# A transformer layer on one core: splitting the second chunk of 512 queries into two of 256

## The chip, the core and the metric

The kernel runs on one core of a Trainium2 chip. The core has a matrix engine (TensorE, PE in the profile, with its weight loads as PEld), a vector engine (VectorE, DVE), an activation engine (ScalarE, ACT), a general engine (GpSimd, POOL) and a queue that only issues transfers (SyncE, SP). The metric is device time in microseconds (us).

## The reference

The reference is one pre-norm transformer layer on 2048 tokens of width 640, in bfloat16: 32 attention heads of 20 columns, then a gated MLP of width 1728.

```python
qkv = (x @ wqkv).reshape(B, S, 3, H, Dh) ...          # S 2048, D 640, H 32, Dh 20
scores = einsum("bhqd,bhkd->bhqk", q, k) * Dh ** -0.5
o = einsum("bhqk,bhkd->bhqd", softmax(scores), v)
attn = o.reshape(B, S, D) @ wo
h = x + A(layernorm(x))                                # A: attention as above
h2 = h + (gelu(n @ w_gate) * (n @ w_up)) @ w_down      # n = layernorm(h), width 1728
```

## The kernel before

**Chunks and slots.** The queries are cut into chunks (`SIZES`, L308): 512, 512, 256, 256, 256, 128 and 128. The heads are in 8 groups of 4. A slot is the work of one 512-wide block of query columns: one group for a 512 chunk, two groups at once for a 256 chunk, four for a 128 chunk. So there are always 32 slots, 8 for a chunk of 512, 4 for one of 256 and 2 for one of 128.

**Tiles.** A score tile is 128 partitions (keys) by 512 columns in one PSUM bank, and belongs to one head. The four heads of a group lie in four groups of 32 rows of PE (index `j`, `tile_position=(32 * j, 0)` in `qk_mms`, L913), and four tiles with the same place are a quad. A slot has 64 tiles, 2048 in all. For 512 queries a tile is one matmul of 512 columns, for 256 queries two of 256, for 128 four of 128.

**Two exponentials.** Most tiles go to ACT, several banks in one `ACTIVATE` (L945). Some quads (`D_QUADS`, L323: 1 to 3 a slot, 68 quads or 272 tiles in all) go to DVE, which reads a tile out of PSUM (L852) and computes the exponential by a chain of six integer and half-precision operations (L863 to L868, in the helper's line L354 in the profile) on two tiles at once, or on four from slot 18 on. 1776 tiles are left for ACT.

**Units and banks.** A unit is what one `ACTIVATE` takes. `PAT` (L798) gives the banks: banks 0 to 2 and 3 to 4 in turn, so that units have three and two tiles, except in chunk 1, where banks 0 to 2 and 3 to 5 are used. There a unit that also carries a DVE tile has two tiles for ACT and puts the DVE tile in its third bank ("six"). Elsewhere the DVE tile gets a bank of its own out of `BG[c]` (L1156): the banks of 7, 5 and 4 that `PAT` leaves. That is bank 7 alone in chunk 1, and 7 and 5 elsewhere. The DVE tiles are taken in a fixed order (`dq`, L793), row groups 0, 1, 2, 3 of a quad one after the other, whatever row groups the tiles of the unit use.

**Values.** The products with v (`pv_op`, L875) gather in bank 6. At the end of a slot `epilogue` (L997) copies the bank out (`osb`), transposes it, divides, and writes `o_nat`.

**After a chunk.** `post(c, ...)` (L1036) does the rest for the queries of a chunk: transposes, the output projection (L640), the residual (L1057), layernorm statistics and apply, then for each 512 columns a gate matmul (L1089) with its copy out of PSUM (L1124), GELU on ACT for the whole chunk at once (`after=cp`), the up matmul (L1089 again) with its product (L1135), and the down matmul (L1146) with its residual sum (L1150) and the output transfer. It runs in the gaps of the next chunk, in the banks `BG[c + 1]`. The GELU uses another function table of ACT than exp, so each chunk costs a table load before and one after. The last chunk is the `tail`, with all banks and GELU bank by bank (L1111). Chunks share buffers: `base(c)` (L991) gives the first of four row tiles (`h_sb`, `o_nat`, `hnT`, and the stretch of `ha_f` from `hb`). A chunk of 512 takes all four, the chunks of 256 take 0 to 1 or 2 to 3 in turn. A chunk's `post` therefore waits until the chunk that held its tiles before has read them for the last time.

**Order of the work.** Nothing is queued by hand: `Sched` (L44) is a list scheduler in the program that simulates the engines with fixed costs and writes out a fixed order for each engine. Priorities (L329 to L330): scores 0, values 1, `P_EPI` 2 (the DVE exponential too), `P_LN` 2.5 (projection and layernorm of `post`), `P_BG` 3 (its MLP); among equals the earlier chunk goes first. DVE operations that free a bank have at most 1.8. GELU on ACT has -1. PE is filled with idle matmuls (L354, `ps<-kt_all,zer`) where the planner finds it too quiet. The planner takes 0.215 us for a unit's scores and 0.08 us for a DVE tile's, whichever row groups they use.

Of the kernel before, what the change touches and what calls it, by code (L numbers as in the profile page):

```python
# [304 lines left out]
NT = S // 128  # L305
NA = D // 128
NG = H // 4
SIZES = (512, 512, 256, 256, 256, 128, 128)  # L308
CHUNKS = tuple((sum(SIZES[:i]), n) for i, n in enumerate(SIZES))
NF = (DFF + 127) // 128  # L310
F0 = tuple(min(128 * f, DFF - 128) for f in range(NF))
# [16 lines left out]

P_EV = 1.8  # L329
P_QK, P_PV, P_PRO, P_EPI, P_LN, P_BG = 0, 1, 1.5, 2, 2.5, 3  # L330


def bass_sequential_preLN__mha_block__glu_gated_geglu__prompt_kernel(
# [12 lines left out]
    with ExitStack() as es:  # L346
# [16 lines left out]
        def c_dve(n, rate=1.0625):  # L363
            return 0.061 + n * rate * 1e-3
# [208 lines left out]
        def ln_apply(eng, src, dst, dkey, t, rkeys, prio):  # L573
            if eng == "act":
                fn = I("activation", dst, src, ACT.Identity, bias=nm[:, t:t + 1], scale=rs[:, t:t + 1])
            else:
                fn = I("tensor_scalar", dst, src, mu[:, t:t + 1], rs[:, t:t + 1], ALU.subtract, ALU.mult)
            return op(eng, fn, 0.82 if eng == "act" else c_dve(D, 0.46), prio,
                      reads=list(rkeys) + [("mu", t), ("rs", t)] + ([("nm", t)] if eng == "act" else []), writes=[dkey])
# [215 lines left out]
            tiles += rest  # L795
            slot_end.append(len(tiles))

        PAT = [((0, 1, 2), (3, 4, 5)) if c in (1,) else ((0, 1, 2), (3, 4)) for c in range(len(CHUNKS))]  # L798
        units, ubank, dtile, begins = [], [], [], []
        i, di = 0, 0  # L800
        while i < len(tiles):
            bs = PAT[slots[tiles[i][0]][0]][len(units) % 2]
            six = len(PAT[slots[tiles[i][0]][0]][1]) == 3
            xd = None
            if di < len(dq) and dq[di][0] <= i:
                xd = dq[di][1]
                di += 1
            n = len(bs) - (1 if six and xd else 0)
            units.append(tiles[i:i + n])
            begins.append(i)  # L810
            ubank.append(bs[0])
            dtile.append(xd)
            i += len(units[-1])
        assert di == len(dq)
        d_quad = {}
        for u, x in enumerate(dtile):
            if x:
# [12 lines left out]
        exp_ops = []  # L830
        p_next = [0]

        def d_exp(b, tile, prio, u):

            c = slots[tile[0]][0]
            kind = "e" if c == 0 else "l" if tile[0] < D_WIDE else "w"
            n = 4 if kind == "w" else 2
            h = len(d_raw)
            if h == 0:
                busy = set(x[1][1] for x in d_done)  # L840
                pool = [(kind, i) for i in range(5 if kind != "w" or slots[units[u][0][0]][0] > 3 else 3)]
                pool = [p for p in pool if p not in busy]
                assert pool
                d_cur[0] = min(pool, key=lambda p: d_last.get(p, -1))
                d_last[d_cur[0]] = len(d_ops)
            i = d_cur[0]
            v = {"e": dv0, "l": dv, "w": dvw}[kind][i[1]]
            df, dw = {"e": (df0, dw0), "l": (df1, dw1), "w": (df2, dw2)}[kind]
            keys = [("dv", i)] + ([("dv", ("l", k)) for k in ((0, 1), (2, 3), ())[i[1]]] if kind == "w" and i[1] < 3 else [])
            aft = tuple(e_ops) + (tuple(last_qk[0]) if c else ()) + (tuple(last_qk[1]) + tuple(d_late) if kind == "w" else ()) + \  # L850
                (tuple(last_qk[2]) + tuple(last_qk[3]) if kind == "w" and i[1] > 2 else ())
            d_ops.append(op("dve", lambda eng: eng.tensor_scalar(v[:, 512 * h:512 * h + 512], bank(b), EXP_MUL, -32000.0,  # L852
                                                                 ALU.mult, ALU.max), c_dve(512), P_QK,
                            reads=[("SD", tile)], writes=keys, rel=[b], after=aft))
            d_raw.append(tile)
            if kind != "w":
                d_late[:] = d_ops[-8:]
            if h < n - 1:
                return
            zi = df.bitcast(I16)  # L860
            w_ = len(d_raw) / 2
            d = lambda fn, n, r, w: d_ops.append(op("dve", fn, 0.066 + n * w_, prio, reads=r, writes=w))
            d(I("tensor_scalar", zi, v, 511, 2048, ALU.bitwise_and, ALU.bitwise_or), 0.265, [("dv", i)], ["df"])  # L863
            d(I("tensor_scalar", dw, zi, CA / OCT, CB, ALU.mult, ALU.add), 0.265, ["df"], ["dw"])
            d(I("tensor_tensor", dw, dw, dw, ALU.mult), 0.53, ["dw"], ["dw"])
            d(I("tensor_tensor", dw, dw, zi, ALU.mult), 0.53, ["df", "dw"], ["dw"])
            d(I("tensor_tensor", v, v, dw, ALU.add), 0.53, ["dw", ("dv", i)], [("dv", i)])
            d(I("tensor_scalar", v, v, 0.25, 16256.0 + 128.0 * (CC - 1.0), ALU.mult, ALU.add), 0.265, [("dv", i)], [("dv", i)])  # L868
            if kind != "w":
                d_late[:] = d_ops[-8:]  # L870
            for k, tl in enumerate(d_raw):
                d_done.append((v[:, 512 * k:512 * k + 512].bitcast(BF16), ("dv", i), tl))
            d_raw.clear()
# [115 lines left out]


        def base(c):  # L991
            n = CHUNKS[c][1]
            if n == 128:
                return 2 + (c == len(CHUNKS) - 1)
            return 2 * (c % 2) if n < 512 else 0

        def epilogue(s_, bk):  # L997
            s = s_ % 2
# [35 lines left out]
               after=tuple(e_ops) + tuple(w_readers) if c == 0 else ())  # L1034

        def post(c, banks, tail):  # L1036
            p = P_EPI if tail else P_LN
            q0, nq = CHUNKS[c]
            nt = nq // 128
            tb = base(c)  # L1040
# [2 lines left out]
            for tt in range(tb, tb + nt):  # L1043
                t = q0 // 128 + tt - tb
                i = t % 2
                if tail or c == 0:
                    transposes(o_nat[:, tt, :], [("on", g, tt) for g in range(NG)], oT[:, :, tt * 128:(tt + 1) * 128],
                               ("hnT", tt), banks, P_EPI, "act" if tail else "dve", after=first)
                else:
                    dma_transposes(o_nat[:, tt, :], [("on", g, tt) for g in range(NG)], oT[:, :, tt * 128:(tt + 1) * 128],  # L1050
                                   ("hnT", tt), after=first)
                for hf in range(2):
                    bk = Bank(*banks)
                    key = ("bk", sc_id())
                    list(chain(bk, key, 320, [(oT[:, a, tt * 128:(tt + 1) * 128], wo[:, a, hf * 320:(hf + 1) * 320])
                                              for a in range(NA)], [("hnT", tt), "wo"], p, after=(sc.lw[("h", tt, hf)],)))
                    op("dve", lambda eng, bk=bk, tt=tt, hf=hf, i=i: eng.tensor_tensor(  # L1057
                        h_sb[:, tt, hf * 320:(hf + 1) * 320], bank(bk, 320), h_sb[:, tt, hf * 320:(hf + 1) * 320], ALU.add),
                       c_dve(320), p, reads=[key, ("h", tt, hf)], writes=[("h", tt, hf)], rel=[bk], after=first)
                ln_stats(h_sb[:, tt, :], t, [("h", tt, 0), ("h", tt, 1)], p)  # L1060
            if tail:
                op("act", I("activation", nm[:, 0:1], off0[:, 0:1], ACT.Sqrt), 0.2, -1, mode="sqrt", reads=["off0"],
                   writes=["warmsq"], after=(exp_ops[-1],))
            ln_rsqrt(q0 // 128, nt, p, table=tail)
            if tail:
                op("act", I("activation", nm[:, 1:2], off0[:, 0:1], ACT.Gelu_apprx_tanh), 0.2, -1, mode="gelu",
                   reads=["off0"], writes=["warmge"], after=(sc.lw[("sd16", q0 // 128)],))
            for tt in range(tb, tb + nt):
                t = q0 // 128 + tt - tb
                ln_apply("dve", h_sb[:, tt, :], xn_t[:, t % 2, :], ("xn", t % 2), t, [("h", tt, 0), ("h", tt, 1)], p)  # L1070
                if tail:
                    transposes(xn_t[:, t % 2, :], [("xn", t % 2)], hnT[:, :, tt * 128:(tt + 1) * 128], ("hnT", tt),
                               banks, p, "act", after=first)
                else:
                    dma_transposes(xn_t[:, t % 2, :], [("xn", t % 2)], hnT[:, :, tt * 128:(tt + 1) * 128], ("hnT", tt),
                                   after=first)
# [162 lines left out]
```

## Time and profile before

| | |
|---|---|
| median of 3 runs | 922.22 us (921.98 to 922.87) |
| the profiled execution | 922.3 us, of which the span of its instructions is 920.3 us |
| first and last exponential on ACT | start at 35.4 us, end at 884.7 us |
| exponentials on ACT | 370 of three banks, 333 of two |
| function table loads | 14 |
| granted PE clock | 1.00 |
| ends of the chunks (start of the last `osb` copy) | 245.4, 460.0, 560.0, 667.0, 772.1, 829.3, 886.0 us |

The parts of `post` in the trace, as starts of the first and the last instruction in us:

| chunk (queries) | output projection | gate and up matmuls | GELU | down matmuls | residual sums L1150 |
|---|---|---|---|---|---|
| 0 (512) | 258.4 to 274.2 | 301.4 to 406.0 | 358.9 | 407.1 to 452.6 | 411.6 to 452.9 |
| 1 (512) | 469.2 to 482.4 | 507.9 to 607.0 | 571.0 | 609.5 to 667.8 | 613.4 to 668.2 |
| 2 (256) | 637.9 to 649.4 | 674.1 to 734.8 | 710.2 | 735.9 to 758.4 | 741.4 to 759.1 |
| 3 (256) | 677.9 to 685.9 | 759.5 to 805.3 | 784.2 | 807.9 to 826.7 | 813.6 to 827.0 |
| 4 (256) | 781.6 to 787.3 | 826.8 to 879.5 | 862.4 | 881.5 to 894 | 885.0 to 894.2 |
| 5 (128) | 842.3 to 845.0 | 880.0 to 904 | 897.7 | 904.3 to 908 | 906.4 to 908.3 |
| 6 (128) | 889.8 to 891.1 | to 912.7 | 899.3 to 912.4 | 913.5 to 917.2 | 915.6 to 917.5 |

How to read the profile: a line of the groups has the source line, engine, operation, output and inputs by the names in the program, their shapes and a count, then the busy time in us and the mean duration of one in ns, and at last the idle time before them with what ended it. Durations overlap in a pipeline: two ACT instructions of 1513 and 1096 ns follow each other in less time than that. A line of the timeline has the start, the time until the last of the merged instructions has ended, the engine, and the same names. L354 is the line of a helper that issues many kinds of operation.

### The profile page before, as it was taken

To read this page: it belongs to the slowest core of one execution; us is meant where nothing else is said; L and a number is where in the kernel's file an instruction comes from. 1 tells how busy PE (TensorE), PEld (TensorE's weight loads), DVE (VectorE), ACT (ScalarE), POOL (GpSimd) and SP (SyncE) were. 2 spreads that over 40 slices of the span, in tenths; PEclk is the share of its full clock that TensorE was granted. 3 is DMA by queue.
4 is the path that set the end of the run, shared out by engine and by line. 5 is a ranking of instruction groups with operands and counts; after the bars stand their busy time and mean duration, and the time that the engine had idled before them with its cause. 6 is when DMAs were issued, how large, how long until landed. Compare 5 with 4: busy or idle time off the path is not lost.

```text
span 920.3 us, 23148 instructions
## 1 busy us (share of the span) xinstructions
PE 847.7 (92%) x10202; PEld 356.0 (39%) x10202; DVE 795.2 (86%) x1468; ACT 875.9 (95%) x783; POOL 41.4 (5%) x117
## 2 busy tenths in 40 slices
PE   3999999999898887989998998999999999999998
PEld 2432223222232222223333333344444445666577
DVE  8869898999799996988888999899999888878763
ACT  7899999999999999999999999999999999999961
POOL 5000000000001000000001000000202000100200
PEclk9999999999999999999999999999999999999999
DMA  7311020223801000000122000001120102000000
GB/s 258 94 25 38 12 61 25 84 78 85 293 6 30 1 2 1 1 1 16 44 31 30 2 1 1 1 16 30 22 39 1 16 9 38 17 17 24 10 16 16
DMA packets 39516, 34.36 MB, mean 37 GB/s; under 512 B 19436, under 2 KB 36936, under 8 KB 39416
## 3 DMA queue, kind: packets, MB, share of 16 engines
q1 hardware_dynamic: 39416, 32.89, 13.2%
q8 instruction: 80, 1.31, 0.6%
q14 instruction: 20, 0.16, 0.1%
HBM read 20.12 MB, written 8.09 MB: 31 GB/s over the span
## 4 chain that ended last, share of the span: by engine, by line
ACT 51%; PE 34%; DVE 12%; DMA 1%; issue 0%; SPq 0%; DVEq 0%
ACT pts L354 32%; ACT rege L354 18%; PE ps L917 10%; PE ps L354 7%; PE ps L1089 6%; PE ps L640 6%; DVE qt_all L354 5%; PE ps L1146 4%; DVE qt_all L852 2%; DVE rege L354 2%; DMA regw<-in_A_wqkv_dram 1%; DVE rege L852 1%; ACT L354 1%; PE ps L1012 1%; PE ps L585 1%
## 5 line engine op out<-in xcount | busy, mean ns | idle before, releaser
L354 ACT ACTIVATE pts<-ps 128x1536 bf16<-128x1536 f32 (+1 forms) x471 | 559.3, 1316 | 7.7 <-PE ps L917 5.4
L917 PE MATMUL ps<-qt_all,kt_all 32*128 32x256 bf16 (+2 forms) x3584 | 321.1, 288 | 37.7 <-ACT pts L354 22.8
L354 ACT ACTIVATE rege<-ps 128x1536 bf16<-128x1536 f32 (+1 forms) x232 | 284.9, 1314 | 2.1 <-PE ps L354 1.4
L917 PEld LDWEIGHTS ps<-qt_all,kt_all 32*128 32x128 bf16 x3584 | 104.4, 92 | 259.7 <-ACT pts L354 134.0
L354 DVE TENSOR_TENSOR qt_all<-qt_all 128x2048 f16<-128x2048 f16 (+3 forms) x186 | 175.0, 941 | 2.2
L1089 PE MATMUL ps<-rege,regw 128*128 128x256 bf16 (+2 forms) x980 | 160.9, 290 | 9.9 <-ACT rege L354 3.4
L354 PE MATMUL ps<-pts,v_all 128*21 128x256 bf16 (+2 forms) x2080 | 122.5, 290 | 0.0
L852 DVE TENSOR_SCALAR qt_all<-ps 128x512 int16<-128x512 f32 x128 | 87.7, 685 | 27.2 <-PE ps L917 26.9
L852 DVE TENSOR_SCALAR rege<-ps 128x512 int16<-128x512 f32 x128 | 87.7, 685 | 15.3 <-PE ps L917 14.2
L1089 PEld LDWEIGHTS ps<-rege,regw 128*128 128x128 bf16 x980 | 71.9, 97 | 70.7 <-issue 28.7
L354 PE MATMUL ps<-rege,v_all 128*21 128x256 bf16 (+2 forms) x1204 | 94.5, 295 | 0.2 <-DVE qt_all L354 0.2
L640 PE MATMUL ps<-regw 128*128 128x512 bf16 (+1 forms) x360 | 86.3, 350 | 2.3 <-DMA regw<-in_A_wqkv_dram 0.7
L354 DVE TENSOR_SCALAR qt_all<-qt_all 128x1024 f16<-128x1024 int16 (+2 forms) x153 | 85.0, 560 | 1.8
L1146 PE MATMUL ps<-regw,rege 128*128 128x320 bf16 x448 | 79.0, 301 | 1.7 <-DVE rege L1135 0.6
L354 DVE TENSOR_TENSOR rege<-rege 128x1024 f16<-128x1024 f16 (+4 forms) x106 | 67.4, 647 | 0.9
L354 PE MATMUL ps<-kt_all,zer 128*32 128x512 bf16 x784 | 63.7, 384 | 0.0
L354 PEld LDWEIGHTS ps<-pts,v_all 128*21 128x21 bf16 x2080 | 45.0, 91 | 32.9 <-issue 28.8
L1146 PEld LDWEIGHTS ps<-regw,rege 128*128 128x128 bf16 x448 | 37.3, 97 | 33.8 <-issue 16.2
L354 DVE TENSOR_SCALAR rege<-rege 128x1024 int16<-128x1024 int16 (+2 forms) x117 | 49.2, 443 | 0.9
L1135 DVE TENSOR_TENSOR rege<-rege,ps 128x512 bf16<-128x512 bf16 (+1 forms) x53 | 35.7, 677 | 14.3 <-PE ps L1089 14.1
L640 PEld LDWEIGHTS ps<-regw 128*128 128x128 bf16 x360 | 28.7, 98 | 47.2 <-issue 21.9
L354 PEld LDWEIGHTS ps<-rege,v_all 128*21 128x21 bf16 x1204 | 32.4, 91 | 24.0 <-issue 17.4
(101 smaller groups left out, 563.3 us busy)
## 6 DMA issues: line engine op xcount, KB each, us to landing
rege<-in_A_x_dram SPq DMA_DIRECT2D x6, 640.0 KB, 5.1
q_rows<-regw SPq DMA_DIRECT2D x20, 128.0 KB, 1.7
out_dram<-rege SPq DMA_DIRECT2D x16, 160.0 KB, 1.8
regw<-in_B_w_gate_dram SPq DMA_DIRECT2D x1, 2160.0 KB, 8.1
regw<-in_B_w_up_dram SPq DMA_DIRECT2D x1, 2160.0 KB, 14.5
regw<-in_B_w_down_dram SPq DMA_DIRECT2D x1, 2080.0 KB, 19.7
kt_all<-k_rows SPq DMA_DIRECT2D x12, 160.0 KB
qt_all<-q_rows SPq DMA_DIRECT2D x12, 160.0 KB
```

The costliest lines, as they stand in the source:

```text
L354: return lambda eng: getattr(eng, method)(*args, **kwargs)
L585: op("pe", lambda eng, a=a: eng.transpose(bank16(bk, D)[:, 128 * a:128 * a + 128], src[:, a * 128:(a + 1) * 128], ident[:]), 0.055, prio, ...
L640: yield op("pe", lambda eng, l=l, r=r, k=k: eng.matmul(bank(bk, n), l, r, start=(k == 0), stop=(k == len(steps) - 1)), c_mm(n), prio, mode ...
L852: d_ops.append(op("dve", lambda eng: eng.tensor_scalar(v[:, 512 * h:512 * h + 512], bank(b), EXP_MUL, -32000.0, ALU.mult, ALU.max), c_dve( ...
L917: return lambda eng: eng.matmul(out()[:, kk * nq:(kk + 1) * nq], kt_all[32 * j:32 * j + 32, g, kt * 128:(kt + 1) * 128], qt_all[32 * j:32 ...
L1012: op("pe", lambda eng, tt=tt: eng.transpose(bank(b2)[:, tt * 128:(tt + 1) * 128], osb[:, s, tt * 128:(tt + 1) * 128], identf[:]), c_mm(128 ...
L1089: op("pe", lambda eng, a=a, f=f, fi=fi: eng.matmul(bank(bk)[:, fi * nq:(fi + 1) * nq], w[:, a, F0[f]:F0[f] + 128], hnT[:, a, 128 * tb:128 ...
L1135: hdone.append(op("dve", lambda eng, bu=bu, fv=fv, w=w: eng.tensor_tensor(fv, fv, bank(bu, w), ALU.mult), c_dve(w), p, reads=[ku] + hkeys( ...
L1146: op("pe", lambda eng, f=f, o=o, hf=hf, bk=bk: eng.matmul(bank(bk, 320), ha_f[:, o:o + 128], wd[:, f, hf * 320:(hf + 1) * 320], start=(f = ...
```

## The change

`SIZES` gets eight chunks: the second chunk of 512 becomes two of 256. `BASE` lists each chunk's first row tile. For the chunks from query 1024 on it is the same as before, and the two new chunks take tiles 0 to 1 and 2 to 3. `SIX` is empty, so that all chunks use the banks 0 to 2 and 3 to 4, and 7 and 5 are free for the DVE tile and for `post` everywhere. A unit that is due for a DVE tile now looks at the next four of the list, within the same quad, for a head whose row group none of its own tiles uses. If there is none, it takes no DVE tile, and the next unit looks again. `q_done(k)` and the test on query 1536 keep the former conditions on buffers under the new chunk numbers. `P_LND` and `P_LNP` split the layernorm's priority in two names with the same value 2.5.

```diff
-SIZES = (512, 512, 256, 256, 256, 128, 128)
+SIZES = (512, 256, 256, 256, 256, 256, 128, 128)
+BASE = (0, 0, 2, 0, 2, 0, 2, 3)
+SIX = ()
...
+P_LND, P_LNP = 2.5, 2.5
...
-        PAT = [((0, 1, 2), (3, 4, 5)) if c in (1,) else ((0, 1, 2), (3, 4)) for c in range(len(CHUNKS))]
+        PAT = [((0, 1, 2), (3, 4, 5)) if c in SIX else ((0, 1, 2), (3, 4)) for c in range(len(CHUNKS))]
...
-            if di < len(dq) and dq[di][0] <= i:
-                xd = dq[di][1]
-                di += 1
-            n = len(bs) - (1 if six and xd else 0)
+            n = len(bs)
+            if dq and dq[0][0] <= i:
+                n -= 1 if six else 0
+                js = [x[3] for x in tiles[i:i + n]]
+                q = dq[0][1][:3]
+                fit = [k for k in range(min(4, len(dq))) if dq[k][1][:3] == q and dq[k][1][3] not in js]
+                if fit:
+                    xd = dq.pop(fit[0])[1]
+                elif six:
+                    n += 1
...
+        def q_done(k):
+            return sum((tuple(last_qk[c]) for c, (q0, _) in enumerate(CHUNKS) if q0 // 512 == k), ())
...
-            aft = tuple(e_ops) + (tuple(last_qk[0]) if c else ()) + (tuple(last_qk[1]) + tuple(d_late) if kind == "w" else ()) + \
-                (tuple(last_qk[2]) + tuple(last_qk[3]) if kind == "w" and i[1] > 2 else ())
+            aft = tuple(e_ops) + (q_done(0) if c else ()) + (q_done(1) + tuple(d_late) if kind == "w" else ()) + \
+                (q_done(2) if kind == "w" and i[1] > 2 else ())
...
         def base(c):
-            n = CHUNKS[c][1]
-            if n == 128:
-                return 2 + (c == len(CHUNKS) - 1)
-            return 2 * (c % 2) if n < 512 else 0
+            return BASE[c]
```

More of the change, by code (lines that the diff above doesn't have):

```diff
@@ L796, in bass_sequential_preLN__mha_block__glu_gated_geglu__prompt_kernel @@
             slot_end.append(len(tiles))
-        PAT = [((0, 1, 2), (3, 4, 5)) if c in (1,) else ((0, 1, 2), (3, 4)) for c in range(len(CHUNKS))]
+        PAT = [((0, 1, 2), (3, 4, 5)) if c in SIX else ((0, 1, 2), (3, 4)) for c in range(len(CHUNKS))]
         units, ubank, dtile, begins = [], [], [], []
-        i, di = 0, 0
+        i = 0
         while i < len(tiles):
@@ L813, in bass_sequential_preLN__mha_block__glu_gated_geglu__prompt_kernel @@
             i += len(units[-1])
-        assert di == len(dq)
+        assert not dq
         d_quad = {}
@@ L840, in d_exp @@
                 busy = set(x[1][1] for x in d_done)
-                pool = [(kind, i) for i in range(5 if kind != "w" or slots[units[u][0][0]][0] > 3 else 3)]
+                pool = [(kind, i) for i in range(5 if kind != "w" or CHUNKS[slots[units[u][0][0]][0]][0] >= 1536 else 3)]
                 pool = [p for p in pool if p not in busy]
@@ L1036, in post @@
         def post(c, banks, tail):
-            p = P_EPI if tail else P_LN
+            p = P_EPI if tail else P_LNP
+            pd = P_EPI if tail else P_LND
             q0, nq = CHUNKS[c]
@@ L1058, in post @@
                         h_sb[:, tt, hf * 320:(hf + 1) * 320], bank(bk, 320), h_sb[:, tt, hf * 320:(hf + 1) * 320], ALU.add),
-                       c_dve(320), p, reads=[key, ("h", tt, hf)], writes=[("h", tt, hf)], rel=[bk], after=first)
-                ln_stats(h_sb[:, tt, :], t, [("h", tt, 0), ("h", tt, 1)], p)
+                       c_dve(320), pd, reads=[key, ("h", tt, hf)], writes=[("h", tt, hf)], rel=[bk], after=first)
+                ln_stats(h_sb[:, tt, :], t, [("h", tt, 0), ("h", tt, 1)], pd)
             if tail:
@@ L1063, in post @@
                    writes=["warmsq"], after=(exp_ops[-1],))
-            ln_rsqrt(q0 // 128, nt, p, table=tail)
+            ln_rsqrt(q0 // 128, nt, pd, table=tail)
             if tail:
@@ L1069, in post @@
                 t = q0 // 128 + tt - tb
-                ln_apply("dve", h_sb[:, tt, :], xn_t[:, t % 2, :], ("xn", t % 2), t, [("h", tt, 0), ("h", tt, 1)], p)
+                ln_apply("dve", h_sb[:, tt, :], xn_t[:, t % 2, :], ("xn", t % 2), t, [("h", tt, 0), ("h", tt, 1)], pd)
                 if tail:
```

## The prediction

> **What bounds the kernel now.** I read the busy times first, then the busy tenths of the 40 slices.
>
> ```profile
> PE 847.7 (92%) x10202; PEld 356.0 (39%) x10202; DVE 795.2 (86%) x1468; ACT 875.9 (95%) x783; POOL 41.4 (5%) x117
> PE   3999999999898887989998998999999999999998
> DVE  8869898999799996988888999899999888878763
> ACT  7899999999999999999999999999999999999961
> ```
>
> ACT is full from slice 3 to slice 38, then empty. So the time is a start, a full stretch of exponentials that ends at 884.74 us, and a tail of 35.5 us without them. The full stretch is priced by the groups kept apart by shape.
>
> ```profile
> L354 ACT ACTIVATE pts<-ps 128x1536 bf16<-128x1536 f32 x248 | 371.7, 1513 | 6.3 <-PE ps L917 4.0 <-PE ps L354 1.1
> L354 ACT ACTIVATE pts<-ps 128x1024 bf16<-128x1024 f32 x223 | 243.9, 1096 | 1.4 <-PE ps L917 1.4
> L354 ACT ACT_TABLE_LOAD x14 | 18.0, 1283 | 1.0 <-PEq L1224 0.8
> ```
>
> From start to start, undisturbed, three banks take 1.330 us and two 0.904 (tenth percentile of the trace's steps). What the steps have above that sums to 20.8 us, which is all that ACT loses by waiting. A GELU episode in the timeline of ACT (chunk 0's):
>
> ```profile
> 356.11 1.45 ACT L354 ACTIVATE rege<-ps 128x1536 bf16<-128x1536 f32 x1
> 357.58 1.28 ACT L354 ACT_TABLE_LOAD   x1
> 358.87 6.46 ACT L354 ACTIVATE rege<-rege 128x2048 bf16<-128x2048 bf16 x4
> 365.34 1.28 ACT L354 ACT_TABLE_LOAD   x1
> 366.64 1.02 ACT L354 ACTIVATE rege<-ps 128x1024 bf16<-128x1024 f32 x1
> ```
>
> Then the tail, in the timeline of PE after the last exponential:
>
> ```profile
> 885.88 1.12 PE L1146 MATMUL ps<-regw,rege 128*128 128x320 bf16 x7
> ...
> 887.28 1.11 PE L1146 MATMUL ps<-regw,rege 128*128 128x320 bf16 x7
> ...
> 888.80 1.25 PE L1146 MATMUL ps<-regw,rege 128*128 128x320 bf16 x8
> 889.89 1.52 PE L640 MATMUL ps<-wo,rege 128*128 128x320 bf16 x10
> 891.25 2.88 PE L1146 MATMUL ps<-regw,rege 128*128 128x320 bf16 x20
> ...
> 895.64 8.81 PE L1089 MATMUL ps<-rege,regw 128*128 128x128 bf16 x152
> 904.29 3.97 PE L1146 MATMUL ps<-regw,rege 128*128 128x320 bf16 x28
> 908.10 4.80 PE L1089 MATMUL ps<-rege,regw 128*128 128x128 bf16 x83
> 913.48 3.98 PE L1146 MATMUL ps<-regw,rege 128*128 128x320 bf16 x28 [0.58 <-DVE rege L1114]
> ```
>
> The reader is to see that PE has no gap there but one of 0.58 us, and that much of its work is old: the down matmuls until 894 are chunk 4's, and of the 128-column matmuls and the down matmuls at 904.29 a large part is chunk 5's. The table of `post` says why: from 469 us on the chunks' MLPs stand in one queue, chunk 2's begins 114 us after its scores are done, and the queue is still there at the end.
>
> **The tail's price.** Old work after 884.8: 42 down matmuls at 0.142 us (28 in 3.97) are 6.0; chunk 5's 140 gate and up matmuls, less the 13 done before, at 0.058 (152 in 8.81) are 7.4; its 28 down matmuls 4.0; together 17.4 us. The last chunk's own chain (values, copy, transposes, projection, layernorm) needs until 895.6 whatever PE does, and uses some 3.6 us of PE in it, so about 7.4 us of old work fit there free. Without old work beyond that: 895.8 + 140 x 0.058 + 0.6 + 4.0 = 908.5 as the end of PE, and 2.8 us for the last sum and transfer as now (917.46 to 920.26). The tail would be 26.6, say 27.2 with slack for the alternation of gate, GELU and up. Each us of old work over 7.4 costs about one.
>
> **Part 1, the split (ACT).** One more GELU episode: two loads of 1.283, some 0.2 of waiting at its edges (0.25, 0.23 and 0.16 at three episodes), and 2 x 3.29 for 6.46 of GELU: +2.9 us, on ACT, hidden by nothing. [...]
>
> **Part 2, 3+2 banks (ACT).** 1776 tiles are now 370 + 333 units. In threes and twos alone they are 355 + 355 and one of a single tile: 472.2 + 320.9 + 0.5 against 492.1 + 301.0, +0.4 us.
>
> **Part 3, 256 for 512 columns on PE and DVE.** A 3-tile score unit takes 324 ns from its first matmul to the next other one with 512 columns and 326 with 256. Gate and up: 0.11 for 0.2155 halved, +0.6 us over the 140. Evacuations stay 14 + 14, SP's transposes stay one per row tile, and a prefetch and one chain of small POOL operations (0.35 us each) come in, which only the layernorm waits for. In the epilogues two products of 313 ns stand for one of 485, 1.1 us of DVE over eight slots. All lies in slots 8 to 15, where from 280 to 460 us PE runs 0.4 to 1.8 us in 20 of idle matmuls and DVE is at 12.7 to 19.5 of 20: nothing on the path. If that cover were gone, under 2 us.
>
> **Part 4, free row groups (PE).** Score matmuls in one row group follow each other, those in different ones overlap. Two units in chunk 1:
>
> ```profile
> 329.95 0.60 PE L917 MATMUL ps<-qt_all,kt_all 32*128 32x512 bf16 x3
> 330.48 0.61 PE L1089 MATMUL ps<-rege,regw 128*128 128x512 bf16 x2
> 331.03 0.39 PE L917 MATMUL ps<-qt_all,kt_all 32*128 32x512 bf16 x3
> ```
>
> Three matmuls take 0.60 where two share a row group and 0.39 where none do: 0.21 us. By the list in the code 171 of 272 DVE tiles meet their own row group in their unit, and in the trace 150 of the 643 groups of two to four tiles take over 0.5 us. The change takes away 171 x 0.21 = 36 us of PE. Little is directly on ACT: steps with a slow group in the 2.4 us before them lose 36 ns on average, the others 23, so 253 x 0.012 = 3 us at most. I take 1.5, bounds 0 and 6 (a third of what is lost). The rest is PE time for the queue of MLPs, about 4 us in 100. The price: a DVE tile may be put off by up to two units of 1.13 us, and the products at the slot's end wait behind it on PE, with the next scores queued behind them; the lead of 24 tiles (11 us) covers it against a chain of 5.7 us (0.68 + 0.68 + 1.22 + 1.22 + 1.21 + 0.68).
>
> **Part 5, the queue moves forward.** Chunk 1's MLP starts now at 507.9: scores end at 460, projection at 469, layernorm until 503 with PE idle. After: the first half's scores end near 348 and its row tiles are free after chunk 0's fourth residual sum (429.9), so projection and layernorm lie beside chunk 0's down matmuls, and its MLP starts when those end, near 453. That is 55 us earlier. With 160 us for the 512 queries as now, the two halves end at 613 (668 now); then 84 to 697, 67 to 764; the next chunk's scores end at 772, its layernorm some 30 later, 67 more to 870 (894 now); the first chunk of 128 then has until 888. At 4.7 us a bank (seven gate banks in 33 us) its four gate banks are done at 889. So old work left: up 4.1 and down 4.0, perhaps 1 of gate: 9, of which 7.4 are free. Tail 28.5 for 35.5.
>
> **The sum** (case A): 884.74 + 2.9 + 0.4 - 1.5 = 886.5; + 28.5 = 915.0; + 2.04 outside the span (922.3 against 920.26) = **917.1 us**. The profiled execution stands 0.1 above the median of 922.22. From about 920.4 to 924.1 is within 0.2%, which is what a measurement of this kernel can't tell from no change.
>
> **Rivals.**
> *B: the queue gets further still, and the first 128 chunk's GELU runs before the last exponential.* It then costs ACT an episode that it shares with the tail today: 2.8 + 1.7 of GELU (1792 columns, 897.7 now). The tail is 27.2: 884.74 + 3.3 - 1.5 + 4.5 + 27.2 + 2.0 = 920.3; without the 1.5 us, 921.8. The 889 above is so near the end, and the 36 us of PE help so much, that this is nearly as likely.
> *C, slower: the old work stays.* DVE is at 18 to 19.9 of 20 from 500 to 580 us, and layernorm (2.5) stands behind the DVE exponentials (2). If the two new layernorms wait there so long that the queue reaches the tail as it does now, only the costs are left: 884.74 + 3.3 + 35.5 + 2.0 = 925.6. It decides from a tail over 34.0, that is over 14 us of old work, with ACT's waits unchanged. Against it: the first half's layernorm moves to 430 to 450 us, where DVE is at 16.
> *D, slower: DVE tiles come too late at slot ends.* ACT's worst waits, 1.68 us after 138 and 1.51 after 693.7, stand at slot ends where PE waits for DVE. Ten slots with two or three quads each are tight; from A four such stops end at 923, six at 926.
> *E: ACT's waits shrink by up to 6*: A gives 912.6.
> That the split changes nothing but order can't be: the extra chunk has its GELU.
>
> **How the numbers follow.** A 0.38 (913 to 920: 0.36 faster, 0.02 same), B 0.30 (0.14 faster, 0.16 same), C 0.17 (0.13 slower, 0.04 same), D 0.10 slower, E 0.05 faster. Faster 0.55, same 0.22, slower 0.23. The range 912 to 926 leaves out half of E and the far part of D; A's own is 913 to 920.
>
> **What the profile after would show.** Table loads: 16 in A, 18 in B, not 14. Score groups over 0.5 us gone. 711 exponentials. Down matmuls for the second 256 queries before 540 us. After the last exponential, 56 down matmuls or little more in place of 100, and a tail of 27 to 29. Wrong would make me: a tail of 34 or more (part 5), or ACT waiting clearly more than 20.8 us (part 4's put-off tiles).

## The result, and the profile after

The changed kernel takes 926.32 us (median; 925.25 to 928.33) against 922.22: a ratio of 1.0040, 95% interval 1.0029 to 1.0052. It is slower by 4.1 us, where 5.1 us less were forecast. The time lies just outside the range. The profiled execution is the slowest of them, 928.3 us with a span of 926.4. Beside it stands a second profile, from the same kernel run again beside the experiments (span 925.2), where one number could mislead. Medians here are of the fast executions alone: two of `rows_only` below, 1734 and 2103 us, are left out.

The page after, its busy times and slices, looks much as before. In the row of the PE clock one digit is an 8:

```profile
PE 855.1 (92%) x11280; PEld 387.6 (42%) x11280; DVE 794.5 (86%) x1477; ACT 881.6 (95%) x795; POOL 43.7 (5%) x131
...
PE   3999999999898999999989989989999989989998
...
DVE  7959999989799996879968998999799998798663
ACT  6799999999999999999999999999999999999972
...
PEclk9999999999999999999989999999999999999999
```

ACT is full from the same slice to the same slice. The groups by shape give the new units, 355 of each size, and 18 table loads in place of 14:

```profile
L357 ACT ACTIVATE pts<-ps 128x1536 bf16<-128x1536 f32 x237 | 361.7, 1526 | 7.3 <-PE ps L929 4.1 <-PE ps L357 2.9
L357 ACT ACTIVATE pts<-ps 128x1024 bf16<-128x1024 f32 x237 | 261.8, 1105 | 1.6 <-PE ps L357 1.4 <-PE ps L929 0.2
L357 ACT ACT_TABLE_LOAD x18 | 23.1, 1283 | 1.1 <-PEq L1234 0.8
```

The last exponential, that of the single tile, is the third of the row before the next table load:

```profile
889.23 2.87 ACT L357 ACTIVATE pts<-ps 128x1536 bf16<-128x1536 f32 x3
892.11 1.28 ACT L357 ACT_TABLE_LOAD   x1
```

It ends at 892.09 us (884.74 before), and the tail takes 34.34 (35.52). So the last exponential comes 7.4 us later and the tail gives back 1.2. The 7.4 by their parts: the first exponential starts 1.0 later (36.37 for 35.37), two more table loads before the last exponential are 2.6, the GELU in two pieces and eight more units 0.5, and ACT's waits, by the same measure as before, 3.0 (23.5 for 20.5). The sum is 7.1.

The split's episode and what follows it, in the timeline of ACT:

```profile
463.33 1.28 ACT L357 ACT_TABLE_LOAD   x1
464.63 3.28 ACT L357 ACTIVATE rege<-rege 128x2048 bf16<-128x2048 bf16 x2
467.93 1.28 ACT L357 ACT_TABLE_LOAD   x1
469.22 2.37 ACT L357 ACTIVATE pts<-ps 128x1536 bf16<-128x1536 f32 x2
473.77 1.45 ACT L357 ACTIVATE rege<-ps 128x1536 bf16<-128x1536 f32 x1 [2.19 <-PE ps L929]
```

The loads take 1.28 us each, as in before (14 with a mean of 1283 ns). The 2.19 us of waiting after them are new. The same stretch in windows of 4 us (busy time of PE, PEld, DVE, ACT and POOL with counts, then the granted PE clock, the DMA share and GB/s):

```profile
460.00:464.00 4.00, 3.43 (x50) 1.59 (x48) 3.93 (x8) 3.98 (x5) 0.00 (x0) 1.00 0.00 0
464.00:468.00 4.00, 2.31 (x9) 1.05 (x9) 1.91 (x6) 3.97 (x4) 0.00 (x0) 0.59 0.21 41
468.00:472.00 4.00, 4.00 (x23) 2.80 (x21) 0.96 (x2) 3.58 (x3) 0.00 (x0) 0.55 0.21 41
472.00:476.00 4.00, 3.69 (x56) 1.91 (x54) 2.02 (x5) 2.23 (x2) 0.00 (x0) 1.00 0.01 4
```

PE's clock is halved there: the granted clock is 0.50 from 464.8 to 471.6 us and 1.00 on both sides, just while 25 up matmuls of the MLP and then the next scores are due. Why PE was quiet is in its own timeline:

```profile
463.84 0.44 PE L1021 MATMUL ps<-identf,osb 128*128 128x128 f32 x2
465.96 1.46 PE L357 MATMUL ps<-kt_all 128*128 128x512 bf16 x3 [1.69 <-DVE o_nat L1030]
467.22 5.03 PE L1099 MATMUL ps<-rege,regw 128*128 128x256 bf16 x25
...
473.33 0.40 PE L929 MATMUL ps<-qt_all,kt_all 32*128 32x256 bf16 x6
```

The GELU falls on the end of a slot. After 463.5 us no scores are made until 473.3, while ACT is busy with the loads and the GELU and reads no score bank, and PE stands with its filling matmuls behind DVE's last step of the slot (`o_nat`). The clock drops 0.5 us into that wait of 1.69. But PE was as quiet where the clock held: in the second profile of after the same place has the same 2.31 of 4 us, and the clock stays at 1.00:

```profile
464.00:468.00 4.00, 2.31 (x22) 1.48 (x17) 2.14 (x6) 3.99 (x3) 0.00 (x0) 1.00 0.16 33
...
466.85 2.89 PE L1099 MATMUL ps<-rege,regw 128*128 128x256 bf16 x25
...
469.46 2.37 ACT L357 ACTIVATE pts<-ps 128x1536 bf16<-128x1536 f32 x2
471.71 2.37 ACT L357 ACTIVATE rege<-ps 128x1536 bf16<-128x1536 f32 x2
```

The 25 matmuls take 2.89 us there in place of 5.03, and ACT doesn't wait. So the 2.19 us are the price of the halved clock, not of the episode. In the first profile there are three half-clock stretches before the last exponential (3.4, 3.4 and 6.8 us, each with a granted clock of 0.50), in the second three of 3.4, two of them at the same places (352 and 414 us) and one at 577.6, in that of before none.

The tail of PE after the last exponential:

```profile
898.02 1.11 PE L1099 MATMUL ps<-rege,regw 128*128 128x128 bf16 x17
...
903.16 2.85 PE L1099 MATMUL ps<-rege,regw 128*128 128x128 bf16 x48 [0.16 <-ACT rege L357]
...
906.13 2.12 PE L1099 MATMUL ps<-rege,regw 128*128 128x128 bf16 x35
908.08 3.97 PE L1156 MATMUL ps<-regw,rege 128*128 128x320 bf16 x28
911.89 7.25 PE L1099 MATMUL ps<-rege,regw 128*128 128x128 bf16 x127
919.66 3.98 PE L1156 MATMUL ps<-regw,rege 128*128 128x320 bf16 x28 [0.52 <-DVE rege L1124]
```

The old work is still there. The MLP of the chunk at query 1536 has its last residual sum at 894.1 us, as before, and the first 128 chunk does its GELU at 901.4 and its up and down matmuls after that. 260 gate and up matmuls of 128 columns (267 before) and 69 down matmuls (98) lie behind the last exponential.

### The profile page after: what moved, and what is told of

It is laid out like the page before. It is cut to its first block, busy times and chain, and to the rows that moved or that the text cites. A ratio compares the mean times of both kernels' runs of the same rounds, so it can differ in the third digit from the quotient of the medians.

```text
span 926.4 us, 25297 instructions
## 1 busy us (share of the span) xinstructions
PE 855.1 (92%) x11280; PEld 387.6 (42%) x11280; DVE 794.5 (86%) x1477; ACT 881.6 (95%) x795; POOL 43.7 (5%) x131
## 4 chain that ended last, share of the span: by engine, by line
ACT 60%; PE 28%; DVE 9%; DMA 2%; issue 0%; SPq 0%; DVEq 0%
ACT pts L357 38%; ACT rege L357 21%; PE ps L929 7%; PE ps L1099 6%; PE ps L643 5%; PE ps L357 5%; PE ps L1156 4%; DVE qt_all L357 3%; DMA regw<-in_A_wqkv_dram 1%; DVE qt_all L864 1%; ACT L357 1%; DVE rege L864 1%; DVE rege L357 1%; DVE rege L1134 1%; PE ps L588 1%; PE ps L1021 1%
## 5 line engine op out<-in xcount | busy, mean ns | idle before, releaser
L357 ACT ACTIVATE pts<-ps 128x1536 bf16<-128x1536 f32 x475 | 559.9, 1314 | 8.9 <-PE ps L357 4.3
L357 ACT ACTIVATE rege<-ps 128x1536 bf16<-128x1536 f32 x236 | 288.8, 1319 | 4.2 <-PE ps L929 4.0
L929 PEld LDWEIGHTS ps<-qt_all,kt_all 32*128 32x128 bf16 x4096 | 109.0, 92 | 246.7 <-ACT pts L357 122.3
L1099 PE MATMUL ps<-rege,regw 128*128 128x256 bf16 (+2 forms) x1120 | 164.0, 279 | 6.9 <-ACT rege L357 1.8
L1099 PEld LDWEIGHTS ps<-rege,regw 128*128 128x128 bf16 x1120 | 86.8, 99 | 66.1 <-issue 33.7
L357 PEld LDWEIGHTS ps<-pts,v_all 128*21 128x21 bf16 x2368 | 54.4, 91 | 31.2 <-issue 26.3
L357 PE MATMUL ps<-kt_all,zer 128*32 128x512 bf16 x676 | 58.0, 386 | 0.0
L357 PEld LDWEIGHTS ps<-rege,v_all 128*21 128x21 bf16 x1392 | 37.7, 91 | 22.9 <-issue 15.1
```

The lines of the kernel that those rows point to most:

```text
L357: return lambda eng: getattr(eng, method)(*args, **kwargs)
L929: return lambda eng: eng.matmul(out()[:, kk * nq:(kk + 1) * nq], kt_all[32 * j:32 * j + 32, g, kt * 128:(kt + 1) * 128], qt_all[32 * j:32 ...
L1099: op("pe", lambda eng, a=a, f=f, fi=fi: eng.matmul(bank(bk)[:, fi * nq:(fi + 1) * nq], w[:, a, F0[f]:F0[f] + 128], hnT[:, a, 128 * tb:128 ...
```

## The experiments

All of them keep the kernel's output. The exception is `one_table`, which says what it leaves out. Half-clock stretches vary between executions of one and the same kernel (the six of after have mean granted clocks of 0.993 to 0.998). The mean clock gives an estimate of their number: in after's profile 13.65 us at 0.50 in a span of 926.4 make 0.993, so 0.998 is about one stretch of 3.4 us, 0.996 two, 0.994 three, 0.993 four (a double one counts twice). Before has none in 51 of the 91 executions beside the experiments, one in 38 and four in two. Three theories run through the expectations: T1, the cost is the GELU episode that the split adds; T2, the cost is a PE that gets through its work sooner with free row groups and so loses its clock; T3, the cost is the new order that any change deals.

### The parts alone

`rows_only`, `banks_only`, `split_no_rows` and `no_split` take the kernel after with parts put back:

```diff
 rows_only:      SIZES and BASE as before, SIX = (1,)
 banks_only:     SIZES and BASE as before, SIX = (),   fit = [0]
 split_no_rows:  new SIZES,                SIX = (),   fit = [0]
 no_split:       SIZES and BASE as before, SIX = (),   row groups chosen
-SIZES = (512, 256, 256, 256, 256, 256, 128, 128)
+SIZES = (512, 512, 256, 256, 256, 128, 128)
-                fit = [k for k in range(min(4, len(dq))) if dq[k][1][:3] == q and dq[k][1][3] not in js]
+                fit = [0]
```

> The kernel before (chunks of 512 and 512, six banks in chunk 1) with the choice of free row groups alone. Theory T1 (the split's extra GELU episode is the loss, and the rest is neutral): 921 to 923 us, 14 table loads, groups of scores over 0.5 us nearly gone. Theory T2 (the row-group choice itself costs, by DVE tiles put off and by a PE so much quieter that its clock is halved for stretches): 924 to 927 us, with some of the granted clock lost.

> The kernel before with 3+2 banks in chunk 1 alone. T1: +0.4 us of units, so 922 to 924, unless the second background bank brings chunk 0's MLP forward. T2 says nothing else. A third theory, T3 (every change re-deals the planner's order, and the tail and the waits move by some us with no cause of their own): anything from 919 to 927.

> The kernel after with the DVE tiles taken in the old fixed order: split and 3+2 banks without the row-group choice. T1: as slow as after, 925 to 927. T2: 922.5 to 924.5, with the granted clock at 1.00. T3: anything from 921 to 929.

> The kernel after with the old chunks: 3+2 banks and row groups, no split. T1: 922 to 923.5, with one GELU episode fewer than after. T2: 924 to 927, like after. T3: anything from 920 to 930.

| | us, median | ratio to before (95%) | last exponential ends | tail |
|---|---|---|---|---|
| rows_only | 923.72 | 1.0012 (0.9997 to 1.0027) | 885.98 | 35.9 |
| banks_only | 927.98 | 1.0055 (1.0039 to 1.0071) | 886.82 | 40.2 |
| split_no_rows | 926.59 | 1.0038 (1.0025 to 1.0052) | 890.06 | 34.0 |
| no_split | 932.89 | 1.0109 (1.0089 to 1.0129) | 892.41 | 37.3 |

My first theory after the result (T1, the split's GELU episode is the loss) falls: the two versions without the split and with 3+2 banks are the slowest. The split takes 1.4 us off `banks_only` and 6.6 off `no_split`. These two lie above every range that was given for them. `rows_only`, with its clock mostly at 0.994, lies between T1 and T2. `split_no_rows` comes out as T1 and T3 had it; T2's 922.5 to 924.5 at full clock misses, since it takes 924.8 even then. In `banks_only` the 3+2 banks cost 2.1 us up to the last exponential and 4.7 in the tail, which is 40.2 us. No direct cause of that is seen in the banks. Chunk 0's MLP is even done earlier with two banks (last residual sum 419.7 for 452.9 us). But the layernorm of the chunk at query 1024 is done at 702 us, not at 665, and the MLPs of this chunk and the next end 32 and 27 us later. That points to T3, a re-dealt order.

### Another order of the same work

```diff
-QK_LEAD = .65
+QK_LEAD = .6        (lead06; .7 in lead07)
```

> The kernel before with one constant of its planner moved that has nothing to do with the change: QK_LEAD, the lead that scores get on PE, 0.60 for 0.65. Same instructions, another order. Theory T3 (the order before is a lucky deal among many, and the change merely re-deals it): clearly slower than 922, 925 to 929 us, with the loss in the tail and no half-clock stretch. Theory T1/T2 (the loss belongs to parts of the change): within 1 us of 922.

> The same with QK_LEAD 0.70. T3: 923 to 928 us. T1/T2: within 1 us of 922.

> The kernel after with QK_LEAD 0.60. T3: anywhere within 922 to 930, as likely better as worse than 926.3; with the two of before it gives two small samples that overlap. T1/T2: within 1 us of 926.3. Either way the half-clock stretches stay, if it is the free row groups that leave PE too quiet.

> The kernel after with QK_LEAD 0.70. T3: anywhere within 922 to 931. T1/T2: within 1 us of 926.3. The half-clock stretches stay.

| | us, median | ratio to before (95%) | last exponential ends | tail |
|---|---|---|---|---|
| before_lead06 | 927.28 | 1.0049 (1.0032 to 1.0067) | 886.01 | 41.2 |
| before_lead07 | 926.29 | 1.0039 (1.0026 to 1.0052) | 884.23 | 39.7 |
| after_lead06 | 926.38 | 1.0039 (1.0024 to 1.0054) | 890.21 | 34.3 |
| after_lead07 | 928.39 | 1.0068 (1.0045 to 1.0091) | 893.33 | 38.1 |

T3 holds. Moving a constant that has nothing to do with the change makes the kernel before as slow as after. The instructions are the same but for 4 to 20 more idle matmuls and, in `before_lead06`, two more table loads in the tail. So the tail of 35.5 us belongs to one order, and its neighbours don't have it. The PE tail of before_lead07, to be laid beside that of before:

```profile
892.32 4.10 PE L1146 MATMUL ps<-regw,rege 128*128 128x320 bf16 x29
...
896.54 3.83 PE L1146 MATMUL ps<-regw,rege 128*128 128x320 bf16 x27
900.21 7.94 PE L1089 MATMUL ps<-rege,regw 128*128 128x128 bf16 x137
```

All 56 down matmuls of chunk 4 lie here in the tail, and its up matmuls before them. In before's order 14 of them are done by the last exponential. The difference begins far earlier: in before chunk 2's layernorm is applied at 661.7 and 664.9 us, in lead06 and lead07 at 689 to 691, and the MLP starts at 674 or at 702 to 703. Taken together, and each from one profile, the six different orders with a second chunk of 512 (`rows_same_order` below shares that of before) have tails of 35.5, 35.9, 40.2, 37.3, 41.2 and 39.7 us, 38.3 on average, and last exponentials at 886.7 on average. The split's four orders with unchanged priorities (after, split_no_rows and the two leads) have tails of 34.3, 34.0, 34.3 and 38.1, 35.2 on average, and last exponentials at 891.4. So in these few orders the split shortens the tail by 3.1 us and ends the exponentials 4.7 us later. Three more (ln_first, split_six_ln and split_proj_first below), with priorities moved to help the MLPs, have tails of 30.8, 30.0 and 32.7, and last exponentials at 892.5.

### The episode's price, and what holds up the MLPs

```diff
 one_table:
-I("activation", fv, fv, ACT.Gelu_apprx_tanh)
+I("activation", fv, fv, ACT.Exp if c == 1 else ACT.Gelu_apprx_tanh)
 ln_first:
-P_LND, P_LNP = 2.5, 2.5
+P_LND, P_LNP = 1.9, 1.9
```

> The kernel after with the GELU of the first half of the old second chunk (queries 512 to 767) computed as exp, so that ACT needs no other function table there; every engine's order stays the same, less two table loads. This leaves the GELU of these queries out. Theory T1 (an episode's loads lie on ACT and nothing hides them): 2.6 us less than after, so 923.5 to 924, 16 table loads, the same tail. If the episode were hidden by something: 926, as after. [...]

> The kernel after with both layernorm priorities of post at 1.9, ahead of the DVE exponentials (2) and of the values' end. Theory T4 (the chunks' MLPs no longer queue behind each other but each waits 39 to 48 us for its own projection and layernorm): MLPs of the chunks from query 1024 on begin 15 to 30 us after the chunk's scores, the first 128 chunk's GELU comes before the last exponential, which moves 4 to 5 us later, and the tail falls to 30 to 32 us; in sum 924 to 928. If the MLPs begin no earlier, T4 is wrong and the wait is for PE or banks.

`one_table` took 925.44 us (1.0023, 1.0010 to 1.0037), 0.9 less than after and not 2.6. Its profile has 16 loads, and from the first exponential to the last 853.5 us against 855.7 and 854.4 in after's two profiles, while ACT's waits are 24.0 us against 23.5 and 22.1. So the two loads are gone, but part of them comes back as waiting. With three half-clock stretches it is no faster than after with three (926.5 and 926.4), with two 0.9 faster (924.8 and 925.7). No further gap is seen at the loads in the rows of after: the GELU starts 0.02 us after the first load has ended (464.63 after 463.33 and 1.28), and the next exponential 0.01 after the second (469.22 after 467.93 and 1.28).

`ln_first` took 926.15 (1.0036, 1.0024 to 1.0048). The MLPs of the chunks from query 1024 on begin at 614, 722 and 819 us, 38, 40 and 32 us after their scores (start of the last `osb` copy), where after has 48, 45 and 39. So the priority takes 5 to 10 us off this wait, which stays at 32 to 40 and doesn't fall to the expected 15 to 30. Most of it is a chain: in after, for the chunk at query 1024, transposes on SP from 584.1 us, the projection with its sums on DVE from 588.9 to 601.8, statistics until 609.6, 14 small operations on POOL until 616.1, the apply and two more transposes until 623.3. The tail fell to 30.8 us, as expected, but the first 128 chunk's GELU stayed behind the last exponential, which ends at 892.70 us, and the median is that of after.

### Two more deals of the split

```diff
 split_six_ln:      SIX = (1, 2), fit = [0], P_LND, P_LNP = 1.9, 2.5
 split_proj_first:  SIX = (),     fit = [0], P_LND, P_LNP = 2.5, 1.9, QK_LEAD = .63, PE_AGE = 1.2
```

> The split, with six banks in both halves as the old chunk 1 had, the DVE tiles in the old order, and the layernorm's DVE part at 1.9. T3 (the order is a deal): this deal has a short tail, 919 to 923 us. T1: not under 924, since it has the extra episode.

> The split with 3+2 banks, the DVE tiles in the old order, the projection's priority on PE at 1.9, and two planner constants moved (QK_LEAD 0.63, PE_AGE 1.2). T3: a deal with an early last exponential, 920 to 924 us. T1: 925 to 927, like the split with 3+2 banks alone.

`split_six_ln` missed: 931.29 (1.0088, 1.0055 to 1.0121). It has the shortest tail of all, 30.0 us, but its last exponential ends at 895.5 and its granted clock went down to 0.983. `split_proj_first` came out as T3 expected, 922.69 (1.0006, 0.9982 to 1.0030), no different from before. So a kernel with the extra episode can take the time of before. What the episode itself costs this doesn't show, since the order and three constants are others.

### Free row groups with the order held

In `rows_same_order` the kernel before keeps its order, instruction for instruction; within a quad the DVE tiles only change places. A tile with a free row group is taken where there is one, otherwise the next, and none is put off. `shared_same_order` does the opposite in the order of after.

```diff
 rows_same_order (the due times stay in their order):
+                same = [k for k in range(min(4, len(dq))) if dq[k][1][:3] == q]
+                fit = [k for k in same if dq[k][1][3] not in js]
+                xd = dq.pop((fit or same)[0])[1]
 shared_same_order (the units that carry a DVE tile stay):
+                j = ([j for j in left if j in js] or left)[0]
```

`split_warm` is a split with more idle matmuls: `WARM_MIN` 0.7 for 0.5, `PAD_MIN` 0.6 for 0.42, `fit = [0]`, `P_LNP` 1.9, `QK_LEAD` 0.6, `PE_AGE` 1.2.

> The kernel before in its own order, instruction for instruction on every engine; only the head of each DVE tile is exchanged within its quad so that its scores use a free row group where there is one, and no tile is put off. Theory T2 (a quieter PE loses its clock): 923 to 925 us, two or more half-clock stretches in a run where before has none or one, though score groups over 0.5 us get much fewer. Step 4 of the prediction: 920 to 922, the waits of ACT 1.5 us less.

> The kernel after in its own order, with the heads of the DVE tiles exchanged the other way, so that they share a row group with a tile of their unit where they can. T2: the granted clock back to 0.998 or 1.00, and 924 to 925.5, faster than after. Step 4 of the prediction: slower than after, 927 to 928.

> The split with 3+2 banks, the DVE tiles in the old order, the projection's priority at 1.9, and more idle matmuls on PE (thresholds 0.7 and 0.6 for 0.5 and 0.42; QK_LEAD 0.60, PE_AGE 1.2). T3 with T2 (a good deal of the order and a held clock): 920 to 922 us, clock 0.998 or 1.00, at or below before. T1 (the split can't pay for its GELU episode): 924 or more.

> The kernel after unchanged, as the measure for the other three on the same chip: 925.5 to 927, granted clock 0.993 to 0.998, and the time rising by about 1.4 us with each half-clock stretch among its own executions.

| | us, median | ratio to before (95%) | clock, mostly |
|---|---|---|---|
| rows_same_order | 920.69 | 0.9971 (0.9960 to 0.9983) | 0.998 |
| shared_same_order | 933.59 | 1.0103 (1.0084 to 1.0123) | 0.993 |
| split_warm | 934.19 | 1.0119 (1.0101 to 1.0137) | 1.000 |
| after_again | 926.59 | 1.0042 (1.0027 to 1.0056) | 0.994 |

`rows_same_order` beats both kernels. The stretch of chunk 1 that the prediction showed, here a little earlier, in the timeline of PE:

```profile
329.04 0.39 PE L927 MATMUL ps<-qt_all,kt_all 32*128 32x512 bf16 x3
329.37 0.60 PE L1099 MATMUL ps<-rege,regw 128*128 128x512 bf16 x2
330.26 0.39 PE L927 MATMUL ps<-qt_all,kt_all 32*128 32x512 bf16 x3 [0.29 <-ACT pts L354]
```

The first group now takes 0.39 us where it took 0.60. Score groups over 0.5 us went from 150 to 109, ACT's waits from 20.5 to 17.9 us, and the tail is the same (35.51 for 35.52). PE spends the time that it has won waiting for ACT (the 0.29 in brackets). `shared_same_order` has 177 such groups (after some 108) and is 7 us slower than after, clearly against T2's expectation. Its profiled execution was the quickest of its six (928.2, clock 0.998), 3.0 us above after's with the same clock (925.2). Where the other 5 us of its usual 933.6 lie isn't shown. `split_warm` held its clock and lost far more. Its page, and the slices of PE:

```profile
PE 904.7 (97%) x12290; PEld 412.5 (44%) x12290; DVE 799.7 (86%) x1477; ACT 890.1 (95%) x795; POOL 41.9 (4%) x131
...
PE   3999999999999999999999999999999999999998
```

1696 idle matmuls (676 in after) make PE full, and ACT waits 33.0 us.

The last pair does the same exchange in the order of two splits:

```diff
+                j = ([j for j in left if j not in js] or left)[0]
 split_rows_now:   in the order of split_no_rows
 split_proj_rows:  in the order of split_proj_first
```

> The split with 3+2 banks in exactly the order of split_no_rows (926.6 us), with the heads exchanged within their quad for free row groups and no tile put off: all three ideas of the change, less the putting off. If free row groups gain wherever the order is held, 1.5 to 3 us less than split_no_rows: 923.5 to 925, which is also 1 to 3 less than after. If the gain was peculiar to the order of before: 926 to 927.5.

> The same exchange in exactly the order of split_proj_first (922.7 us). Expected 919.5 to 921.5, at or below rows_same_order (920.7), so that the split is no loss in a good order. If the split can't pay for its GELU episode: 922 or more.

| clock (half-clock stretches) | 1.000 (0) | 0.998 (1) | 0.996 (2) | 0.994 (3) | 0.993 (4) | 0.991 (5) | median |
|---|---|---|---|---|---|---|---|
| before, all runs | 922.1 | 924.3 | | | | | 922.2 to 923.0 |
| rows_same_order | 920.4 | 920.7 | 921.3 | | | | 920.69 |
| split_no_rows | 924.8 | 927.3 | 928.8 | | | | 926.59 |
| split_rows_now | 923.1 | 925.2 | 928.2 | 928.0 | | 931.4 | 926.54 |
| split_proj_first | 920.5 | 922.4 | 923.8 | | | | 922.69 |
| split_proj_rows | | 921.8 | 923.3 | 923.9 | 926.1 | | 923.34 |
| after | | 925.2 | 925.7 | 926.4 | 928.3 | | 926.32 |

The cells are medians of the executions with that clock, often of one to five. The splits and their exchanged forms ran on different chips, on which before differs by up to 0.3 us at full clock. Left out are two executions of before at 0.993 and 0.992 (927.2 and 927.3) and one of split_proj_first at 0.985 (932.7).

The medians missed both expectations (split_rows_now: ratio 1.0043, 1.0025 to 1.0060; split_proj_rows: 1.0008, 0.9994 to 1.0021) and lie where the other readings had put them, 926 to 927.5 and 922 or more: no gain. The table says why. At an equal number of half-clock stretches free row groups are faster in all three orders, by 1.7 us without a stretch in the order of before (922.1 to 920.4), by 0.7 to 2.1 in that of split_no_rows and by 0.5 to 0.6 in that of split_proj_first. But the stretches become more: split_no_rows has none in half of its executions, split_rows_now in one of twelve, and up to five. In the split's order that eats the gain. In the order of before, one stretch costs 2.2 us, and only 0.3 with free row groups. So T2 is half right: with free row groups the clock was lost more often in these three orders (before has no stretch in 51 of 91 executions and rows_same_order in 2 of 11, split_proj_first in one of ten and split_proj_rows in none of twelve). In the order of after, putting the shared groups back didn't bring the clock back (0.993, mostly), so it isn't the only cause there.

## Why the prediction was wrong

**The failed step is part 5, the queue.** Its first half held, at its end nearly to the microsecond: the two new MLPs start at 441 (453 forecast) and end their down matmuls at 612.7 us (613). Its second half failed. From there the sum let each MLP start when the one before ended, or 30 us after its scores. In fact each waits for its own chunk: 624.8, 727.4 and 825.1 us, which is 48, 45 and 39 us after the start of the chunk's last `osb` copy. And the scores themselves end later: those up to query 1792 at 785.9 us, where the sum kept 772 from before. The rows of after for the chunk at query 1536, in the timelines of DVE and PE: the copy at the end of its scores, the last apply of its layernorm, the first gate matmuls and the last residual sum:

```profile
785.91 0.68 DVE L357 COPY osb<-ps 128x512 f32<-128x512 f32 x1
...
819.85 0.44 DVE L357 TENSOR_SCALAR xn_t<-rege,mu,rs 128x640 bf16<-128x640 bf16 x1
...
825.11 0.50 PE L1099 MATMUL ps<-rege,regw 128*128 128x256 bf16 x3
...
894.08 0.49 DVE L1160 TENSOR_TENSOR rege<-ps,rege 128x320 bf16<-128x320 f32 x1 [1.41 <-PE ps L1156]
```

The later scores are the point I missed. The GELU that moves forward moves onto ACT, ahead of scores. By 772 before, ACT had done GELU for 1280 queries with six loads. By 786 after, it had done 1536 queries with ten. That is 5.1 us of loads and 3.3 of GELU, and with 1.0 at the start, 0.9 for the units and 2.7 of waits up to there it makes 13 of the 14. So the last 256 chunk's MLP ran from 825 to 894 us as if nothing had changed (the sum had it end at 870: 14 of the difference are the later scores, 9 the longer wait for layernorm), and the tail gave 1.2 us of the 7.0 in the sum. (By its own terms, 27.2 and 9 less 7.4, the sum's tail is 28.8 and not 28.5.)

**Part 1** (+2.9) and **part 2** (+0.4): the loads, the GELU and the 355 + 355 + 1 units are in the trace at that size. Taking two loads away again returned only 0.9 of 2.6 in the median.

**Part 3** (nothing): PE and DVE have room there in the trace; no run tried it alone.

**Part 4** (-1.5): right by itself, -1.7 with the order held (920.69 against 922.44 beside it). In after it wasn't by itself: tiles put off, new banks and new chunks give another order, with GELU episodes on slot ends and a PE whose granted clock fell to 0.993 to 0.998. ACT's waits rose by 3.0 (by 1.6 in the second profile, which lacks the stretch at 464.8). This is the second term with a wrong sign. The 36 us of PE time that were to help the queue were far too many too: with the order held PE's busy time fell from 847.7 to 840.5 us, by 7.2, and 109 of the 150 slow groups stayed. The price of putting tiles off was looked for at slot ends (rival D). `rows_only`, which has it, is 3.0 us slower than `rows_same_order`, which hasn't, but it ran on another chip and also has another order, so the putting off alone isn't separated.

**The rivals.** C named the time (925.6) and the sign: the old work stays. But its mechanism, new layernorms waiting at 430 to 450 us, isn't what happened. They were quick, and the later ones were late. B's early GELU of the first 128 chunk didn't come: it has its loads in the tail, at 898.9 and 903.1 us. E's shrinking waits are out, since they grew.

**What stood behind all of it**: I compared with before as if its tail were what such a kernel has. Other orders of the same work have 39.7 and 41.2 us. Against the orders tried here part 5 has the right sign at under half its size, since the split's tails are 3.1 us shorter on average. Against the one order at hand little was left to gain.

## What to carry to other kernels

Where a planner writes the order, a change of structure also re-deals it, and one tuned order can be the best of many. Re-deal the kernel before by an unrelated constant first: here that alone moved it by 4 to 5 us, as much as the change did. To test a local idea, hold the order and exchange only what the idea is about (the row groups of the scores, -1.7 us in before's order). And work that is pulled forward lands ahead of something: follow which later step it delays, and let every later start in the sum move with it.

## What the runs showed of the hardware

In after PE's clock was halved at 413.6 us (granted clock 0.50 until 417.0, 1.00 before), although PE had been busy for most of the time. From 409 to 413 us PE was busy for 2.97 of 4 us, and its longest gap before the drop was 0.94 us:

```profile
409.00:413.00 4.00, 2.97 (x47) 1.30 (x41) 3.22 (x8) 4.00 (x5) 0.00 (x0) 1.00 0.24 84
413.00:417.00 4.00, 3.77 (x41) 1.48 (x41) 2.90 (x6) 3.46 (x4) 0.00 (x0) 0.57 0.00 0
```

Of the 2.97 us, 1.34 (24 of the 47 matmuls) were scores (`32*128` in the trace). In the second profile of after PE was busy for 2.79 of the 3.40 us before the drop at 577.6, and it kept its clock from 464 to 468 us with 2.31 of 4. So PE's busy time alone doesn't tell when the clock drops; what does stays open. The stretches of after's profile take 3.41, 3.41 and 6.83 us, those of the second profile 3.4 each. What one stretch costs differs from kernel to kernel, by the table of clocks: 2.5 us in split_no_rows, 2.2 in before, 0.3 in rows_same_order, about 1.7 in split_rows_now, 0.6 for the second and the third in after.
